# Chunk attention and phase mixing on one core: three steps moved in the body, and the last tiles' transposes and stores dealt out anew

## The chip, the cores and the metric

The kernel runs on one core of a Trainium2 chip. The metric is device time in microseconds for one execution. Five engines work side by side, each through its own list of instructions in order: TensorE (PE in the profile, its weight loads PEld), VectorE (DVE), ScalarE (ACT), GpSimd (POOL) and SyncE (SP). SP, ACT and POOL can issue DMAs; 16 DMA engines carry them.

## The reference

Attention within chunks of 64 rows, then a mixing layer over the tokens and one over the channels. B = 8, H = 8 heads, S = 576 rows, D = 64, so 512 channels.

```python
scores = scale * np.matmul(q_c, k_c.transpose(0, 1, 2, 4, 3))   # chunks of 64 rows
attn = softmax(scores)
x = np.matmul(attn, v_c)                                        # to [B, S, H * D]
theta = x @ w_theta
zr, zi = x * np.cos(theta), x * np.sin(theta)
y = einsum('ts,bsd->btd', w_tok_r, zr) + einsum('ts,bsd->btd', w_tok_i, zi)
u = x + y
out = u + np.maximum(u @ w_ch, 0.0)
```

Inputs and output are float32; the kernel computes in float16 with float32 sums.

## The kernel before

The eight batches are taken in four pairs p = 0 to 3. A pair has nine tiles of 128 rows: four of its first batch (j = 0 to 3), four of the second (j = 4 to 7), and tile 8 (MID), which holds the last 64 rows of both. For loading and attention the tiles go in groups: A and B are two tiles each of the first batch, C and D of the second, M is tile 8.

All work is cut into steps, and one list, `ORDER`, names them in the order in which they are written out. The list sets each engine's order, since an engine runs its instructions in the order of the list. A step is `kind.pj` or `kind.pG`, with a number behind it for its PSUM bank or buffer slot. `R.32.1` is kind R for pair 3, tile 2, into output buffer 1; `W.38.4` is kind W for pair 3, tile 8, into bank 4. Loads run far ahead of the work of their pair. The kinds that matter here:

- `qk`, `v`: loads of q, k and v, cast to float16 on the way, on POOL's queue (lines 174, 169, 214).
- `T`: 32 by 32 transposes of q and k on DVE (321). `S`: scores on PE (339). `E`: exponential on ACT (365). `V0`, `V1`: attention times v on PE, four heads each (382). `N0`, `N1`: division by the sum on DVE, into x (397, 399).
- `X` and `xa`, `xv`, `xd`: x transposed, by PE with a copy by ACT or DVE, or by a transposing DMA on SP's queue (436).
- `H`: x times w_theta on PE (457), called the phase product here. `G`: cosine and sine on ACT (476). `Z`: zr and zi on DVE (492 to 499).
- `Y`: the mix over tokens on PE, 9 matmuls a tile, 18 for MID (522). `A`: u = x + y on DVE (534).
- `U` and `ua`, `uv`: u transposed by PE into PSUM (539) and copied by ACT (551) or DVE (549). `ud` does the same with one transposing DMA on SP's queue (547).
- `W`: u times w_ch on PE, four matmuls (562), the channel product. For the very last tile it is cut into two halves, W0 and W1. `R`: out = u + max(product, 0) on DVE (574), the sum of the title.
- `st`, `sa`: the store of a tile's output from SP's queue or from ACT's (590; 587 for MID, which takes two DMAs). `st0` and `sa1` store the halves of the last tile.

PSUM has eight banks, used by number. Output buffers o0 to o5 are used by slot: an R that writes slot 4 waits until the store of the R before it in slot 4 has landed. A store issued in order on ACT's or SP's queue waits for its R, and what stands behind it in the queue waits as well.

The end of the list before, from tile 28's store on, shows the order of the stores (ACT's `sa`, SP's `st` and `ud`):

```
sa.33 W.35.5 ud.31.7 ud.38.4 R.35.2 sa.30 sa.28 sa.34 W.36.7 R.36.3 ud.37.2 sa.35 sa.36
W.31.3 R.31.5 W.38.4 R.38.0 W.22.1 R.22.4 sa.31 sa.32 sa.22 W0.37.2 R0.37.2 W1.37.0
st.38 R1.37.3 sa1.37 st0.37
```

Of the kernel before, what the change touches and what calls it, by code (L numbers as in the profile page):

```python
# [17 lines left out]
pre.00 qk.0M.0 hq.0A.1 cqa.0A.2 hk.0A.3 Tq.0M.0 Tk.0M v.0M init.00 v.0A dm.21.7 S.0M.0
E.0M.0 lw.02.4 qk.0B.5 dm.3.7 V1.0M.1 lw.01.6 v.0B ckv.0A lw.00.7 qk.0C.8 Tq.0A.1 Tk0.0A
Tk1.0A dm.1.7 S0.0A.2 S1.0A.4 E0.0A.1 lw.03.9 v.0C qk.0D.10 v.0D E1.0A lc.00 qk.1A.11  # L20
v.1A N1.0M dm.1.7 V0.0A.6 N0.0A V0.0M.0 V1.0A.1 N1.0A dm.3.5 TW.02.3 lt.00.12 X0.0A.5
lt.01.1 twv.02 X1.0A.6 xv0.0A.0 cta.01 xv1.0A cta.00 dm.2.7 H0.0A.7 Tq.0B.2 Tk0.0B
Tk1.0B N0.0M H1.0A.1 S1.0B.2 G0.0A.0 G1.0A Z0.0A dm.1.7 S0.0B.4 Z1.0A TW.01.6 X.0M.0
Ya.02.1 xv.0M.1 twv.01 E0.0B.2 V0.0B.4 N0.0B qk.1M.0 E1.0B V1.0B.6 N1.0B H.0M.0 Ya.01.2
X0.0B.3 X1.0B.4 TW.00.5 xv0.0B.2 G.0M.1 xa1.0B H0.0B.7 H1.0B.0 Tq.0C.0 G0.0B.2 G1.0B
Tk.0C S.0C.3 twv.00 Ya.00.7 Z0.0B TW.03.5 Z1.0B Z.0M Yb.02 Ym.02 E.0C.3 Yb.00 Ym.00 A.02
Yb.01 Tq.0D.1 V1.0C.3 twa.03 A.00 V0.0C.0 Ym.01 Ya.03.5 Tk.0D N1.0C S.0D.6 U.02.3 N0.0C
ua.02.0 qk.1B.3 Yb.03 v.1M lw.04.2 X.0C.4 A.01 U.01.0 Ym.03 qk.1C.1 U.00.1 v.1B E.0D.0
A.03 V1.0D.2 N1.0D ua.01.1 qk.1D.4 qk.2M.12 v.1D V0.0D.6 xa.0C.3 v.2D qk.2C.5 v.1C
W.02.0 N0.0D H.0C.4 U.03.2 ua.00.2 G.0C.0 T.1A.2 W.00.3 R.00.0 X.0D.1 S.1A.6 xv.0D.0  # L30
E.1A.1 v.2B qk.2A.6 W.01.3 H.0D.4 v.2M V0.1A.6 R.02.1 V1.1A.0 R.01.2 Ym.07.3 uv.03.3
G.0D.2 Ym.06.2 Z.0C N1.1A Ya.07 Ym.04.0 Ya.04 Ya.06 N0.1A W.03.1 X.1A.6 xa.1A.1 Z.0D
Yb.06 T.1M.0 Yb.04 TW.04.4 R.03.3 twa.04 T.1B.1 S.1M.7 st.02 E.1M.2 A.04 A.06 S.1B.0
Yb.07 H.1A.4 V1.1M.6 qk.3M.7 qk.2B.8 v.2A A.07 N1.1M E.1B.3 V1.1B.2 st.01 V0.1B.0 N0.1B
Y.08.7 V0.1M.6 N1.1B G.1A.1 U.06.0 ua.06.4 Ym.05.1 N0.1M X.1B.4 st.00 U.04.5 Ya.05
U.07.2 X.1M.3 xa.1B.2 A.08 T.1D.2 xv.1M.3 ua.04.5 H.1B.6 H.1M.0 v.3A qk.3A.9 ua.07.6
W.07.4 qk.3B.10 T.1C.0 G.1B.0 v.2C S.1C.2 S.1D.5 U.08.7 Yb.05 Z.1A Z.1B G.1M.2 Z.1M
uv.08.7 R.07.4 Y.12.0 E.1D.0 Y.11.7 v.3M A.12 E.1C.1 A.05 qk.3C.11 V0.1D.4 T.2M.1
V1.1D.2 V0.1C.0 Y.13.6 N1.1D W.08.2 N0.1D U.12.3 N0.1C A.11 X.1D.4 R.08.5 st.03 uv.12.0
T.2A.0 Y.10.5 A.10 A.13 V1.1C.0 S.2M.7 v.3C qk.2D.0 S.2A.2 N1.1C U.11.5 st.07 uv.11.2  # L40
W.06.6 st.08 X.1C.0 W.04.1 xa.1D.0 H.1D.4 E.2A.3 E.2M.2 R.04.1 U.05.2 xa.1C.1 T.2B.2
G.1D.1 H.1C.0 uv.05.1 T.2C.1 W.05.3 Z.1D st.04 R.05.2 S.2B.4 V1.2M.7 G.1C.0 Z.1C V0.2M.2
E.2B.0 sa.05 N1.2M W.11.3 U.10.0 ua.10.3 Y.17.1 N0.2M R.11.0 R.06.3 A.17 Y.15.7 V0.2B.4
V0.2A.2 A.15 N0.2B N0.2A V1.2B.0 Y.18.6 A.18 S.2C.4 sa.11 X.2M.7 xv.2M.2 W.10.2 N1.2B
R.10.4 E.2C.1 T.3M.0 H.2M.3 Y.16.6 U.13.7 G.2M.2 X.2B.4 V1.2A.0 A.16 st.06 st.10 uv.13.6
xa.2B.3 V0.2C.2 V1.2C.5 N1.2A N1.2C N0.2C W.13.7 R.13.5 sa.13 X.2A.4 xd.2C.0 xv.2A.1
H.2B.0 U.18.5 U.17.6 U.16.2 uv.16.7 U.15.3 Y.14.7 ua.18.4 T.2D.2 Z.2M ua.17.5 ua.15.1
W.16.4 H.2A.5 G.2B.1 S.3M.2 S.2D.0 Z.2B G.2A.0 W.12.3 E.3M.2 R.16.1 A.14 Z.2A U.14.4
W.18.7 R.12.2 R.18.0 Y.21.5 Y.23.6 E.2D.0 st.18 V0.2D.2 T.3C.1 A.21 ua.14.2 v.3B T.3A.0
V1.2D.0 qk.3D.3 N1.2D N0.2D T.3B.2 sa.12 S.3A.4 W.14.7 sa.16 A.23 xd.2D.2 H.2C.0 E.3A.3  # L50
R.14.3 Y.22.4 G.2C.2 V0.3M.5 V1.3M.2 T.3D.0 A.22 Z.2C N1.3M st.14 S.3B.6 E.3B.1 S.3C.0
H.2D.3 E.3C.0 N0.3M W.15.6 Y.20.7 v.3D G.2D.1 ud.23.3 R.15.4 V0.3B.0 V0.3A.5 V1.3A.2
Z.2D A.20 W.17.4 R.17.5 N0.3B Y.24.7 Y.27.4 N1.3A N0.3A A.27 V1.3B.0 xd.3M.3 N1.3B st.15
A.24 V1.3C.2 N1.3C S.3D.5 Y.28.4 V0.3C.0 ud.20.6 E.3D.2 V0.3D.5 V1.3D.2 A.28 H.3M.7
N0.3C N0.3D N1.3D xd.3A.1 G.3M.0 ud.27.7 W.27.4 Y.25.0 xd.3B.0 H.3A.5 A.25 ud.22.0
Y.26.1 G.3A.2 H.3B.2 ud.21.4 st.17 A.26 R.27.0 xd.3C.2 G.3B.1 H.3C.5 Z.3A W.21.7 xd.3D.3
Z.3M ud.24.2 G.3C.2 Z.3B R.21.2 Z.3C H.3D.0 Y.33.4 W.24.2 Y.31.3 sa.21 R.24.1 A.33
G.3D.0 Z.3D Y.32.5 st.27 Y.34.6 A.34 Y.36.7 st.24 ud.25.1 W.25.0 A.32 A.36 ud.33.5
W.33.1 ud.26.7 R.33.3 W.20.2 W.23.4 W.26.6 A.31 R.23.4 R.25.5 ud.32.4 W.32.5 Y.30.7
sa.23 R.20.0 Y.38.1 Y.35.3 ud.34.2 sa.25 R.26.2 R.32.1 W.34.4 A.30 sa.20 A.35 st.26  # L60
ud.28.1 ud.36.5 W.28.0 R.34.4 ud.30.6 ud.35.3 A.38 W.30.2 R.30.5 R.28.0 Y.37.6 A.37
sa.33 W.35.5 ud.31.7 ud.38.4 R.35.2 sa.30 sa.28 sa.34 W.36.7 R.36.3 ud.37.2 sa.35 sa.36
W.31.3 R.31.5 W.38.4 R.38.0 W.22.1 R.22.4 sa.31 sa.32 sa.22 W0.37.2 R0.37.2 W1.37.0
st.38 R1.37.3 sa1.37 st0.37
""".split()


# [1 line left out]
def kernel(  # L69
# [500 lines left out]
    def relu_add(f):  # L570
        def last(p, j, slot):
            ps = st.pop(("ps_w", p, j, f))
            o = buffer([P, DM], "o", slot, FP32)[:, 0 : ps.shape[1]]
            nc.vector.scalar_tensor_tensor(  # L574
                out=o, in0=ps, scalar=0.0, in1=st["x", p][:, j, cols[f]],
                op0=ALU.max, op1=ALU.add,
            )
# [4 lines left out]
    def store(queue, f):
        def put(p, j):
            o = st.pop(("o", p, j, f))
            if j == MID:
                for b in range(2):
                    queue.dma_start(out[2 * p + b, KT * P : S, :], o[half[b]])
            else:
                t0 = (j % KT) * P
                queue.dma_start(out[2 * p + j // KT, t0 : t0 + P, cols[f]], o)  # L590

        return put
# [66 lines left out]
```

## Time and profile before

| | |
|---|---|
| median of 3 runs | 194.25 us (192.99 to 195.4) |
| the profiled execution | 192.63 us, of it 190.9 us from the first to the last instruction (the span) |
| PE busy | 179.3 us, 94% of the span |
| DVE busy | 136.8 us, 72% |
| ACT busy | 100.7 us, 53% |
| POOL busy | 84.9 us, 44%, all of it before 115 us |
| granted TensorE clock | 0.999 |
| DMA moved | 31.48 MB, mean 165 GB/s |

A row of the timeline gives the start and length in us, the engine, the line of the kernel, the operation, what it writes and reads, and how many instructions stand in the row; in brackets, how long the engine was idle before it and what ended that. An engine name with a q (SPq, ACTq) is its sequencer, issuing a DMA. A row of one source line gives the shortest, median and longest duration in ns, and a last line the time of its DMAs from issue to landing. The chain of waits is followed back from the last instruction.

### The profile page before, as it was taken

To read this page: it belongs to the slowest core of one execution; us is meant where nothing else is said; L and a number is where in the kernel's file an instruction comes from. 1 tells how busy PE (TensorE), PEld (TensorE's weight loads), DVE (VectorE), ACT (ScalarE), POOL (GpSimd) and SP (SyncE) were. 2 spreads that over 40 slices of the span, in tenths; PEclk is the share of its full clock that TensorE was granted. 3 is DMA by queue.
4 is the path that set the end of the run, shared out by engine and by line. 5 is a ranking of instruction groups with operands and counts; after the bars stand their busy time and mean duration, and the time that the engine had idled before them with its cause. 6 is when DMAs were issued, how large, how long until landed. Compare 5 with 4: busy or idle time off the path is not lost.

```text
span 190.9 us, 6053 instructions
## 1 busy us (share of the span) xinstructions
PE 179.3 (94%) x2626; PEld 93.0 (49%) x2626; DVE 136.8 (72%) x254; ACT 100.7 (53%) x129; POOL 84.9 (44%) x119
## 2 busy tenths in 40 slices
PE   7769899999999999998999999999989999999980
...
DMA  5999999999999999999999998632498315256596
GB/s 156 252 225 187 176 172 174 193 132 159 259 199 162 120 162 198 183 173 194 201 228 200 176 163 180 85 86 82 84 87 177 99 55 137 59 192 165 133 319 213
DMA packets 99867, 31.48 MB, mean 165 GB/s; under 512 B 90880, under 2 KB 94848, under 8 KB 99840
## 3 DMA queue, kind: packets, MB, share of 16 engines
...
q8 instruction: 20, 0.33, 0.7%
q14 instruction: 7, 0.06, 0.1%
...
## 4 chain that ended last, share of the span: by engine, by line
PE 64%; DMA 17%; POOL 6%; ACT 5%; DVE 3%; issue 3%; DVEq 0%; POOLq 0%
PE psum L522 29%; DMA land<-in_k_dram 15%; PE psum L562 12%; PE psum L457 11%; PE psum L339 4%; POOL v L214 3%; PE psum L382 2%; POOL land L174 2%; DMA uT<-x 2%; PE psum L419 2%; PE psum L539 2%; ACT L144 1%; PE psum L288 1%; DVE T L321 1%; ACT sin L476 1%
## 5 line engine op out<-in xcount | busy, mean ns | idle before, releaser
L522 PEld LDWEIGHTS <-wT 128*128 128x128 f16 (+1 forms) x360 | 31.0, 100 | 34.5 <-issue 1.2
L214 POOL DMA_DIRECT2D v<-in_v_dram x56 | 42.0, 772 | 7.1 <-DMA land<-in_k_dram 4.0
L522 PE MATMUL psum<-zr,wT 128*128 128x512 f16 (+1 forms) x180 | 44.7, 380 | 0.0
L522 PE MATMUL psum<-zi,wT 128*128 128x512 f16 (+1 forms) x180 | 42.9, 379 | 0.0
L534 DVE TENSOR_TENSOR x<-psum,x 128x512 f16<-128x512 f32 x36 | 24.3, 684 | 20.2 <-PE psum L522 20.0
L562 PE MATMUL psum<-wch,uT 128*128 128x512 f16 (+1 forms) x148 | 35.2, 374 | 1.2 <-DMA uT<-x 0.7
L457 PE MATMUL psum<-wtheta,xT 128*128 128x512 f16 x144 | 34.1, 379 | 0.2 <-DVE xT L442 0.2
L321 DVE STREAM_TRANSPOSE T<-land 128x1024 f32<-128x1024 f32 (+4 forms) x27 | 25.4, 953 | 10.0 <-DMA land<-in_q_dram 5.9
L574 DVE SCALAR_TENSOR_TENSOR o<-psum,x 128x512 f32<-128x512 f32 (+1 forms) x37 | 24.1, 670 | 9.3 <-PE psum L562 9.2
L365 ACT ACTIVATE eT<-psum 128x1024 f16<-128x1024 f32 (+1 forms) x22 | 18.2, 860 | 22.7 <-PE psum L339 20.3
L476 ACT ACTIVATE cos<-psum,pihalf 128x1024 f16<-128x1024 f32 (+1 forms) x22 | 21.1, 958 | 12.5 <-PE psum L457 11.4
L399 DVE TENSOR_TENSOR x<-psum,recip 128x512 f16<-128x512 f32 (+1 forms) x40 | 25.5, 638 | 1.4
L144 ACT ACT_TABLE_LOAD x20 | 25.7, 1283 | 1.1 <-PEq L643 0.7
L562 PEld LDWEIGHTS <-uT 128*128 128x128 f16 x148 | 13.6, 98 | 15.8 <-DMA uT<-x 1.5
L457 PEld LDWEIGHTS <-xT 128*128 128x128 f16 x144 | 13.5, 98 | 16.0 <-DVE xT L442 0.6
L476 ACT ACTIVATE sin<-psum 128x1024 f16<-128x1024 f32 (+1 forms) x22 | 19.0, 865 | 0.0
L174 POOL DMA_DIRECT2D land<-in_q_dram x15 | 14.3, 950 | 5.8 <-DMA land<-in_k_dram 2.1
L339 PE MATMUL psum<-T 32*64 32x64 f16 x1152 | 13.7, 193 | 3.3 <-DVE T L321 3.3
L339 PEld LDWEIGHTS <-T 32*64 32x64 f16 x1152 | 11.8, 106 | 7.6 <-DVE T L321 4.3
L174 POOL DMA_DIRECT2D land<-in_k_dram x15 | 13.6, 907 | 1.7 <-DMA land<-in_k_dram 1.5
L492 DVE TENSOR_TENSOR zr<-x,cos 128x1024 f16<-128x1024 f16 (+1 forms) x18 | 11.2, 623 | 1.3 <-ACT cos L476 1.0
L493 DVE TENSOR_TENSOR zi<-x,sin 128x1024 f16<-128x1024 f16 (+1 forms) x18 | 11.3, 627 | 0.8 <-ACT sin L476 0.7
...
## 6 DMA issues: line engine op xcount, KB each, us to landing
...
```

The source lines that it names most:

```text
L144: nc.scalar.activation(out=first, in_=pihalf, func=func)
L174: nc.gpsimd.dma_start(t[:, w].rearrange("p h s d -> p h (s d)"), ap[2 * p + bb, :, s0 : s0 + GT, :].rearrange("h (p s) d -> p h (s d)", s=2),)
L214: nc.gpsimd.dma_start(v16[rows, slot + t, :, 0:D], v[b, :, t0 : t0 + m, :].rearrange("h s d -> s h d"),)
L321: nc.vector.transpose(to.bitcast(FP32).rearrange("p (x l s) -> p x s l", l=32, s=2), src.bitcast(FP32).rearrange("p (x s d) -> p x s d", s ...
L339: nc.tensor.matmul(ps[half[r ^ cc], r, h - hs[0]], t[quarter[c], 1, h, :, e], t[quarter[c], 0, h, :, e], start=(e == 0), stop=(e == 1), ti ...
L399: nc.vector.tensor_tensor(out=x.rearrange("p r (h d) -> p r h d", h=H // 2), in0=ps[:, :, :, 0:D], in1=recip[:, 0:n].broadcast_to((P, n, H ...
L457: nc.tensor.matmul(ps[:, (j - js[0]) * DM : (j - js[0] + 1) * DM], xT[:, j, a, :], wtheta16[:, a, :], start=(a == 0), stop=(a == NDB - 1),)
L476: nc.scalar.activation(out=t[:, js[0] : js[-1] + 1].rearrange("p j e -> p (j e)"), in_=ps, func=AF.Sin, bias=bias, scale=1.0,)
L522: nc.tensor.matmul(ps[half[c]] if j == MID else ps, wT[:, kt, t0 : min(t0 + P, S)], z, start=(b is not None and i == 0), stop=(i == len(kt ...
L534: nc.vector.tensor_tensor(out=x, in0=st.pop(("ps_y", p, j)), in1=x, op=ALU.add)
L562: nc.tensor.matmul(ps, uT[:, a, :], wch16[:, a, cols[f]], start=(a == 0), stop=(a == NDB - 1),)
L574: nc.vector.scalar_tensor_tensor(out=o, in0=ps, scalar=0.0, in1=st["x", p][:, j, cols[f]], op0=ALU.max, op1=ALU.add,)
```

## The change

No step computes anything else than before; the order, three places and some issuers change:

- `R.06.3` stands behind `R.04.1` rather than behind `R.11.0`, and `W.11` writes bank 6 rather than bank 3.
- `H.3M.7` stands ahead of `V0.3C`, `V0.3D` and `V1.3D` rather than behind them.
- Tile 37: `ud.37.2` is gone; `U.37.0` on PE and `ua.37.2` on ACT do its work, behind `W.36`.
- `W.22` stands ahead of `W.38`, and R.22 ahead of R.38.
- Stores: 33, 32, 34, 30 and 28 go from ACT's queue to POOL's (`sg`), each right behind its R or one W later; 35 and 31 go from ACT's to SP's (`st`); the two DMAs of 38 go to SP's and ACT's (`sx`); 36, 22 and the halves of 37 stay where they were.

```diff
-... U.05.2 ... W.11.3 U.10.0 ua.10.3 Y.17.1 N0.2M R.11.0 R.06.3 A.17 ...
+... R.06.3 U.05.2 ... W.11.6 U.10.0 ua.10.3 Y.17.1 N0.2M R.11.0 A.17 ...
-... Y.28.4 V0.3C.0 ud.20.6 E.3D.2 V0.3D.5 V1.3D.2 A.28 H.3M.7 N0.3C ...
+... Y.28.4 H.3M.7 V0.3C.0 ud.20.6 E.3D.2 V0.3D.5 V1.3D.2 A.28 N0.3C ...
+W.25.0 A.32 A.36 ud.33.5 W.33.1 ud.26.7 R.33.3 W.20.2 W.23.4 sg.33 W.26.6 A.31 R.23.4 R.25.5
+ud.32.4 W.32.5 Y.30.7 sa.23 R.20.0 Y.38.1 Y.35.3 ud.34.2 sa.25 R.26.2 R.32.1 sg.32 W.34.4 A.30
+sa.20 A.35 st.26 ud.28.1 ud.36.5 W.28.0 R.34.4 sg.34 ud.30.6 ud.35.3 A.38 W.30.2 R.30.5 sg.30
+R.28.0 sg.28 Y.37.6 A.37 W.35.5 ud.31.7 ud.38.4 R.35.2 st.35 W.36.7 U.37.0 ua.37.2 R.36.3 sa.36
+W.31.3 R.31.5 st.31 W.22.1 W.38.4 R.22.4 sa.22 R.38.0 sx.38 W0.37.2 R0.37.2 st0.37 W1.37.0
+R1.37.3 sa1.37
@@
-    def store(queue, f):
+    def store(queue, f, second=None):
         def put(p, j):
             o = st.pop(("o", p, j, f))
             if j == MID:
-                for b in range(2):
-                    queue.dma_start(out[2 * p + b, KT * P : S, :], o[half[b]])
+                for b, q in enumerate((queue, second or queue)):
+                    q.dma_start(out[2 * p + b, KT * P : S, :], o[half[b]])
@@
+        "sg": store(nc.gpsimd, None), "sx": store(nc.sync, None, nc.scalar),
```

More of the change, by code (lines that the diff above doesn't have):

```diff
@@ L17 @@
 ORDER = """
[L18 to L64, printed above, removed]
+pre.00 qk.0M.0 hq.0A.1 cqa.0A.2 hk.0A.3 Tq.0M.0 Tk.0M v.0M init.00 v.0A dm.21.7 S.0M.0 E.0M.0
+lw.02.4 qk.0B.5 dm.3.7 V1.0M.1 lw.01.6 v.0B ckv.0A lw.00.7 qk.0C.8 Tq.0A.1 Tk0.0A Tk1.0A dm.1.7
@@ new lines @@
+S0.0A.2 S1.0A.4 E0.0A.1 lw.03.9 v.0C qk.0D.10 v.0D E1.0A lc.00 qk.1A.11 v.1A N1.0M dm.1.7
+V0.0A.6 N0.0A V0.0M.0 V1.0A.1 N1.0A dm.3.5 TW.02.3 lt.00.12 X0.0A.5 lt.01.1 twv.02 X1.0A.6
+xv0.0A.0 cta.01 xv1.0A cta.00 dm.2.7 H0.0A.7 Tq.0B.2 Tk0.0B Tk1.0B N0.0M H1.0A.1 S1.0B.2 G0.0A.0
+G1.0A Z0.0A dm.1.7 S0.0B.4 Z1.0A TW.01.6 X.0M.0 Ya.02.1 xv.0M.1 twv.01 E0.0B.2 V0.0B.4 N0.0B
+qk.1M.0 E1.0B V1.0B.6 N1.0B H.0M.0 Ya.01.2 X0.0B.3 X1.0B.4 TW.00.5 xv0.0B.2 G.0M.1 xa1.0B
+H0.0B.7 H1.0B.0 Tq.0C.0 G0.0B.2 G1.0B Tk.0C S.0C.3 twv.00 Ya.00.7 Z0.0B TW.03.5 Z1.0B Z.0M Yb.02
@@ new lines @@
+Ym.02 E.0C.3 Yb.00 Ym.00 A.02 Yb.01 Tq.0D.1 V1.0C.3 twa.03 A.00 V0.0C.0 Ym.01 Ya.03.5 Tk.0D
+N1.0C S.0D.6 U.02.3 N0.0C ua.02.0 qk.1B.3 Yb.03 v.1M lw.04.2 X.0C.4 A.01 U.01.0 Ym.03 qk.1C.1
+U.00.1 v.1B E.0D.0 A.03 V1.0D.2 N1.0D ua.01.1 qk.1D.4 qk.2M.12 v.1D V0.0D.6 xa.0C.3 v.2D qk.2C.5
+v.1C W.02.0 N0.0D H.0C.4 U.03.2 ua.00.2 G.0C.0 T.1A.2 W.00.3 R.00.0 X.0D.1 S.1A.6 xv.0D.0 E.1A.1
+v.2B qk.2A.6 W.01.3 H.0D.4 v.2M V0.1A.6 R.02.1 V1.1A.0 R.01.2 Ym.07.3 uv.03.3 G.0D.2 Ym.06.2
+Z.0C N1.1A Ya.07 Ym.04.0 Ya.04 Ya.06 N0.1A W.03.1 X.1A.6 xa.1A.1 Z.0D Yb.06 T.1M.0 Yb.04 TW.04.4
@@ new lines @@
+R.03.3 twa.04 T.1B.1 S.1M.7 st.02 E.1M.2 A.04 A.06 S.1B.0 Yb.07 H.1A.4 V1.1M.6 qk.3M.7 qk.2B.8
+v.2A A.07 N1.1M E.1B.3 V1.1B.2 st.01 V0.1B.0 N0.1B Y.08.7 V0.1M.6 N1.1B G.1A.1 U.06.0 ua.06.4
+Ym.05.1 N0.1M X.1B.4 st.00 U.04.5 Ya.05 U.07.2 X.1M.3 xa.1B.2 A.08 T.1D.2 xv.1M.3 ua.04.5 H.1B.6
+H.1M.0 v.3A qk.3A.9 ua.07.6 W.07.4 qk.3B.10 T.1C.0 G.1B.0 v.2C S.1C.2 S.1D.5 U.08.7 Yb.05 Z.1A
+Z.1B G.1M.2 Z.1M uv.08.7 R.07.4 Y.12.0 E.1D.0 Y.11.7 v.3M A.12 E.1C.1 A.05 qk.3C.11 V0.1D.4
+T.2M.1 V1.1D.2 V0.1C.0 Y.13.6 N1.1D W.08.2 N0.1D U.12.3 N0.1C A.11 X.1D.4 R.08.5 st.03 uv.12.0
@@ new lines @@
+T.2A.0 Y.10.5 A.10 A.13 V1.1C.0 S.2M.7 v.3C qk.2D.0 S.2A.2 N1.1C U.11.5 st.07 uv.11.2 W.06.6
+st.08 X.1C.0 W.04.1 xa.1D.0 H.1D.4 E.2A.3 E.2M.2 R.04.1 R.06.3 U.05.2 xa.1C.1 T.2B.2 G.1D.1
+H.1C.0 uv.05.1 T.2C.1 W.05.3 Z.1D st.04 R.05.2 S.2B.4 V1.2M.7 G.1C.0 Z.1C V0.2M.2 E.2B.0 sa.05
+N1.2M W.11.6 U.10.0 ua.10.3 Y.17.1 N0.2M R.11.0 A.17 Y.15.7 V0.2B.4 V0.2A.2 A.15 N0.2B N0.2A
+V1.2B.0 Y.18.6 A.18 S.2C.4 sa.11 X.2M.7 xv.2M.2 W.10.2 N1.2B R.10.4 E.2C.1 T.3M.0 H.2M.3 Y.16.6
+U.13.7 G.2M.2 X.2B.4 V1.2A.0 A.16 st.06 st.10 uv.13.6 xa.2B.3 V0.2C.2 V1.2C.5 N1.2A N1.2C N0.2C
@@ new lines @@
+W.13.7 R.13.5 sa.13 X.2A.4 xd.2C.0 xv.2A.1 H.2B.0 U.18.5 U.17.6 U.16.2 uv.16.7 U.15.3 Y.14.7
+ua.18.4 T.2D.2 Z.2M ua.17.5 ua.15.1 W.16.4 H.2A.5 G.2B.1 S.3M.2 S.2D.0 Z.2B G.2A.0 W.12.3 E.3M.2
+R.16.1 A.14 Z.2A U.14.4 W.18.7 R.12.2 R.18.0 Y.21.5 Y.23.6 E.2D.0 st.18 V0.2D.2 T.3C.1 A.21
+ua.14.2 v.3B T.3A.0 V1.2D.0 qk.3D.3 N1.2D N0.2D T.3B.2 sa.12 S.3A.4 W.14.7 sa.16 A.23 xd.2D.2
+H.2C.0 E.3A.3 R.14.3 Y.22.4 G.2C.2 V0.3M.5 V1.3M.2 T.3D.0 A.22 Z.2C N1.3M st.14 S.3B.6 E.3B.1
+S.3C.0 H.2D.3 E.3C.0 N0.3M W.15.6 Y.20.7 v.3D G.2D.1 ud.23.3 R.15.4 V0.3B.0 V0.3A.5 V1.3A.2 Z.2D
@@ new lines @@
+A.20 W.17.4 R.17.5 N0.3B Y.24.7 Y.27.4 N1.3A N0.3A A.27 V1.3B.0 xd.3M.3 N1.3B st.15 A.24 V1.3C.2
+N1.3C S.3D.5 Y.28.4 H.3M.7 V0.3C.0 ud.20.6 E.3D.2 V0.3D.5 V1.3D.2 A.28 N0.3C N0.3D N1.3D xd.3A.1
+G.3M.0 ud.27.7 W.27.4 Y.25.0 xd.3B.0 H.3A.5 A.25 ud.22.0 Y.26.1 G.3A.2 H.3B.2 ud.21.4 st.17 A.26
+R.27.0 xd.3C.2 G.3B.1 H.3C.5 Z.3A W.21.7 xd.3D.3 Z.3M ud.24.2 G.3C.2 Z.3B R.21.2 Z.3C H.3D.0
+Y.33.4 W.24.2 Y.31.3 sa.21 R.24.1 A.33 G.3D.0 Z.3D Y.32.5 st.27 Y.34.6 A.34 Y.36.7 st.24 ud.25.1
+W.25.0 A.32 A.36 ud.33.5 W.33.1 ud.26.7 R.33.3 W.20.2 W.23.4 sg.33 W.26.6 A.31 R.23.4 R.25.5
```

## The prediction

> **What bounds the kernel now.** I read the page first: the busy shares, the DMA line, and the chain that ended last.
>
> ```profile
> PE 179.3 (94%) x2626; PEld 93.0 (49%) x2626; DVE 136.8 (72%) x254; ACT 100.7 (53%) x129; POOL 84.9 (44%) x119
> ...
> DMA  5999999999999999999999998632498315256596
> GB/s 156 252 225 187 176 172 174 193 132 159 259 199 162 120 162 198 183 173 194 201 228 200 176 163 180 85 86 82 84 87 177 99 55 137 59 192 165 133 319 213
> ...
> PE 64%; DMA 17%; POOL 6%; ACT 5%; DVE 3%; issue 3%; DVEq 0%; POOLq 0%
> ```
>
> TensorE (PE) carries 64% of the chain. The DMA engines are full for the first 24 of 40 slices (the loads), and again in the last four (transposes and stores). One slice is 4.77 us. I then cut the second half into stretches with the view by windows (columns: stretch and its length, busy us and count of PE, PE's weight loads, DVE, ACT, POOL, then clock, DMA share, GB/s).
>
> ```profile
> 131.00:157.00 26.00, 25.34 (x262) 12.02 (x260) 18.08 (x37) 12.54 (x15) 0.00 (x0) 1.00 0.52 97
> ...
> 182.00:186.00 4.00, 3.29 (x20) 1.54 (x17) 2.61 (x5) 0.00 (x0) 0.00 (x0) 1.00 1.03 349
> 186.00:190.00 4.00, 0.14 (x2) 0.00 (x0) 0.65 (x2) 0.00 (x0) 0.00 (x0) 1.00 0.80 262
> ```
>
> From 131 us PE has no slack except what these 26 us show (0.66 us). From 182 us the bound changes: PE is idle for 0.7 us, and the DMA engines run full at 349 GB/s. The clock is 1.00 throughout, and POOL does nothing. The chain of the last microseconds and its timeline say which wait ends last.
>
> ```profile
> 179.33 3.98 DMA uT<-x
> ...
> 183.36 1.92 PE psum L562 x8
> ```
>
> ```profile
> 167.79 3.08 DVE L574 SCALAR_TENSOR_TENSOR o<-psum,x 128x512 f32<-128x512 f32 x5 [0.44 <-PE psum L562]
> ...
> 176.29 5.75 SPq L547 DMA_TRANSPOSE uT<-x  x4
> ...
> 178.16 1.29 DVE L574 SCALAR_TENSOR_TENSOR o<-psum,x 128x512 f32<-128x512 f32 x2 [0.44 <-PE psum L562]
> ...
> 179.90 2.75 PE L562 MATMUL psum<-wch,uT 128*128 128x512 f16 x12
> ...
> 180.81 6.22 ACTq L590 DMA_DIRECT2D out_dram<-o  x7
> ...
> 183.36 2.77 PE L562 MATMUL psum<-wch,uT 128*128 128x512 f16 x16 [0.71 <-DMA uT<-x]
> 184.59 2.06 DVE L574 SCALAR_TENSOR_TENSOR o<-psum,x 128x512 f32<-128x512 f32 x4 [1.21 <-PE psum L562]
> ...
> 186.65 0.59 SPq L590 DMA_DIRECT2D out_dram<-o  x1
> ```
>
> By the order, the twelve matmuls at 179.90 are W.35, W.36, W.31; the sixteen at 183.36 are W.38, W.22, W0.37, W1.37. W.38 waits for its transposed tile (ud.38, issued 179.33, landed 183.31). The last R ends at 184.59 + 2.06 = 186.65, SP sends st0.37 then, and the landing takes 3.1 us (row below): 189.75, plus 1.1 us of closing, is the span of 190.9. The seven stores at 180.81 on ACT's queue are 34, 35, 36, 31, 32, 22 and half of 37. Tile 32's result was the last of the five R ending at 170.87, but its store stands fifth in this row: it waits 13 us behind others, and adds its bytes to the full stretch.
>
> **The change part by part.** Body, first place: R.06 moves up behind R.04, and W.11 uses bank 6, which R.06 frees, in place of bank 3, which R.05 frees.
>
> ```profile
> 82.50 0.69 DVE L574 SCALAR_TENSOR_TENSOR o<-psum,x 128x512 f32<-128x512 f32 x1 [1.45 <-PE psum L562]
> 83.97 1.25 DVE L321 STREAM_TRANSPOSE T<-land 128x1024 f32<-128x1024 f32 x1 [0.78 <-DMA land<-in_k_dram]
> ...
> 87.76 0.69 DVE L574 SCALAR_TENSOR_TENSOR o<-psum,x 128x512 f32<-128x512 f32 x1
> 88.36 0.68 DVE L492 TENSOR_TENSOR zr<-x,cos 128x1024 f16<-128x1024 f16 x1
> ```
>
> ```profile
> 88.50 1.02 PE L562 MATMUL psum<-wch,uT 128*128 128x512 f16 x4 [0.49 <-DVE o L574]
> ```
>
> ```profile
> 83.22 9.09 SPq L590 DMA_DIRECT2D out_dram<-o  x2
> ```
>
> DVE: R.04 is the 82.50 row; R.06 behind it needs 0.6 us (five R in 3.08 us: (3.08 - 0.69) / 4) and fits into the 0.78 us in which DVE waits for a landing. Cost nothing; without that cover 0.6 us. PE: W.11's 0.49 us wait for R.05 (87.76 + 0.69) goes. The next product, Y.17, would come 0.49 us earlier at about 89.09, and its first phase input ends at 88.36 + 0.68 = 89.04: just in time. How far does it carry? DVE waits for a landing again:
>
> ```profile
> 107.06 1.25 DVE L321 STREAM_TRANSPOSE T<-land 128x1024 f32<-128x1024 f32 x1 [0.67 <-DMA land<-in_k_dram]
> ...
> 111.75 0.68 DVE L534 TENSOR_TENSOR x<-psum,x 128x512 f16<-128x512 f32 x1
> ...
> 112.65 0.39 PE L539 MATMUL psum<-id,x 128*128 128x128 f16 x4
> ```
>
> From that landing DVE runs without a break to A.14 (111.75 to 112.43), which U.14 on PE needs at 112.65. So only some 0.2 us of the 0.49 survive; I take 0.15, bounds 0 and 0.49. R.06 also issues a store later: st.06 is second in the SP row (ending 92.3) and would go out at about 83.8, since nothing is ahead of it on SP. Its 256 KB then compete with loads 8 us earlier, at 173 to 194 GB/s up to 1.4 us for them. The next landing that DVE waits for is the one at 107.06, and the bytes before that are the same; I take 0, bounds 0.3 either way.
>
> Body, second place: H.3M goes ahead of V0.3C, V0.3D, V1.3D.
>
> ```profile
> 138.84 0.51 PE L382 MATMUL psum<-v,eT 64*64 64x65 f16 x40
> 139.97 0.26 PE L382 MATMUL psum<-v,eT 64*64 64x65 f16 x8 [0.62 <-issue]
> 140.16 1.04 PE L457 MATMUL psum<-wtheta,xT 128*128 128x512 f16 x4
> ```
>
> ```profile
> q8 instruction: 20, 0.33, 0.7%
> ```
>
> PE's work is unchanged (four matmuls), but the 0.62 us stop is not a wait for data: it falls in the middle of V1.3D, and the view gives "issue". The burst runs 40 matmuls in 0.51 us, and queue q8 brings 20 pieces of instructions for 5252 PE entries (2626 loads and matmuls each), about 260 to a piece. I read it as PE running out of instructions. Four slow matmuls ahead of the burst give 0.87 us, more than the stop. Bounds: 0 (it moves along) and 0.62; I take 0.6, since the row is no semaphore wait and the added time covers it. The three V's N's come 0.9 us later on DVE; their users are SP's transposes several us on. The Trainium skill, "Runtime: NRT & Kernel Launch", section "Instruction fetch mechanics", says instructions arrive in 16 KiB blocks of 256 whose boundaries are mostly hidden; by that the stop has another cause, and this term is 0.
>
> The end: tile 37's u goes through PE and ACT rather than through SP's transposing DMA.
>
> ```profile
> 105.10 1.06 PE L539 MATMUL psum<-id,x 128*128 128x128 f16 x16
> ```
>
> ```profile
> L551 ACT COPY uT<-psum x11: 577/587/603, 36.5 to 115.6; 128x512 f16<-128x512 f16 x11
> ```
>
> Four transposes cost PE 0.22 us (1.06 less one matmul's 0.22, over 15, times 4). The copy is 0.59 us on an ACT that has no other work; behind it sa.36 waits, no longer than R.36 makes it wait anyway. U.37 needs A.37, done at 180.79 in time for U.37's place at 181.63. W.22 now goes before W.38, so PE has work while ud.38 lands. On PE: the next slot after W.31 was 182.50 (12 matmuls, 0.216 us each), W.38 began at 183.36; 0.86 lost, less 0.22, is 0.64 us gained: W.31 at 181.85, W.22 182.71, W.38 183.57, W1.37 done at about 185.5.
>
> Stores: 33, 32, 34, 30, 28 go to POOL's queue. No trace row shows a store from POOL; these rows bound its landing.
>
> ```profile
> L214 POOL DMA_DIRECT2D v<-in_v_dram x56: 679/730/950, 3.7 to 107.3; - x56
> ...
> DMA to landing us min/median/max: 3.8/6.6/11.2
> ```
>
> ```profile
> L590 ACTq DMA_DIRECT2D out_dram<-o x8: 338/378/691, 178.9 to 186.7; - x8
> ...
> DMA to landing us min/median/max: 2.7/3.4/4.0
> ```
>
> ```profile
> L590 SPq DMA_DIRECT2D out_dram<-o x1: 591/591/591, 186.6 to 186.6; - x1
> ...
> DMA to landing us min/median/max: 3.1/3.1/3.1
> ```
>
> From 2.7 us (as fast as ACT's) to 11.2 us (POOL's slowest load). I take 4.5, nearest to POOL's fastest 3.8: the loads ran on a full queue, the stores find it empty. It matters, because output buffers come free only on landing: R.31 needs sg.30's, R.22 needs sg.34's, R.38 needs both of sg.28's. R.30 and R.28 end at 178.85 and 179.45; with 0.73 us an issue, the second half of sg.28 is issued at 180.33 and lands at 184.85. R.38 would be ready at 184.6, so it starts at 184.9; R0.37 and R1.37 follow at 0.6 and 0.3 us, and R1.37 ends at 186.25, where before it was 186.65. The store behind it lands in about 2.7 us rather than 3.1, as 0.5 MB (32 and 34) and one 128 KB transpose have left the full stretch: 188.95 against 189.75. Gain 0.8 us. The bounds are +1.5 (3.8 us, no gate, landing 2.3) and a loss (below). The Trainium skill, "DMA: Bandwidth & Descriptors", section "Anatomy of one DMA — SWDGE (gpsimd) path", gives about 2.0 us plus bytes at 436 GB/s; the estimate for 256 KB is 2.6 us, and by it no buffer is late and the tail gains 1.3. No row of POOL here is that fast.
>
> Sum: 0.15 + 0.6 + 0.8 = 1.55 us off the profiled execution's 192.63 us (span 190.9 and 1.7 around it): 191.1, a ratio of 0.992. That execution is 0.8% below the median shown, 194.25; times 0.992 this is 192.7.
>
> **The rivals.** (a) POOL's stores land late, and the result is slower. Every us beyond 4.2 delays R.38, R0.37, R1.37 by one. With the median 6.6: sg.28 lands at 186.95, R1.37 ends at 188.3, its store at 191.3: 1.5 us later than before, 0.8 with the body's 0.75 taken off; 195.0 (with 11.2: 5.4 us, 199.7). It decides from about 5.8 us on. For it: the median is that; against: those loads have small packets on a saturated queue.
>
> (b) The bytes set the end, not the order, and the body's gains are absorbed. DMA share is 1.03 in 182 to 186; then only what the store queues waited counts, some 0.3 us: 193.9. Against it: the 13 us wait of store 32. The Trainium skill's "Issuing engines are not separate DMA queues", in "DMA: Bandwidth & Descriptors", says that spreading over issuers only saves their issue time; by that alone this would be the result.
>
> (c) The early stores slow the transposes.
>
> ```profile
> L547 SPq DMA_TRANSPOSE uT<-x x2: 1222/1222/1222, 179.3 to 180.8; - x2
> ...
> DMA to landing us min/median/max: 4.0/4.1/4.2
> ```
>
> Beside stores a transpose took 4.1 us; ud.31, third of the four from 176.29 (issued about 178.0, now beside sg.34), would land at 182.1, 0.25 us behind W.31's place. At most twice that with ud.30, which takes 0.5 us off the gain: 193.2.
>
> (d) All bounds fall well: 0.49 + 0.6 + 1.5 = 2.6: 191.6.
>
> (e) The moved H.3M only moves the stop, R.06 gains nothing: the tail's 0.8 alone: 193.4.
>
> **How the numbers follow.** Chances: forecast 0.43, (a) 0.15, (b) 0.15, (c) 0.10, (d) 0.09, (e) 0.08. The range 191.2 to 195.1 takes in (b) to (e) and (a) at its median, and leaves out (a)'s far end and luck beyond (d). 2% is 3.9 us, about what a measurement of this kernel can tell from no change: no case but (a) near POOL's slowest gets there, so slower 0.06, faster 0.04, same 0.90.
>
> **What would show it.** PE's 0.49 us before W.11 gone, and U.14 still released by DVE; no "issue" stop in V1.3D; no idle PE between W.31 and W.38; sg landings near 4.5 us; R.38 starting at its buffer's release rather than at its product's end. I am wrong if sg landings exceed 5.8 us, if R.31 waits for sg.30 by more than half a us, or if the stop stands elsewhere in the burst.

## The result, and the profile after

The changed kernel takes 193.29 us (median of 21 runs, 191.55 to 195.67), the kernel before 194.37 us (21 runs, 192.99 to 195.4). The ratio is 0.9937, with a 95% interval of 0.9914 to 0.996. The forecast was 192.7 us, a ratio of 0.992, inside 191.2 to 195.1. It is a gain of 0.6%: well under the 2% that the prediction names as about what can be told from no change, but the interval of the ratio leaves no change out. The ratios here and below leave out executions more than 1.5% above the fastest of their kernel (3 of the 21 of the changed kernel, 6 of 12 of the kernel called "changed, ud.37 back" below), so a ratio is not the quotient of two medians.

The profiled execution of the changed kernel is not a typical one: its span is 192.3 us, longer than the 190.9 us shown of before, mostly because the clock was granted lower early on. So stretches are compared here, not spans. First the page of the changed kernel (busy shares, the clock in 40 slices, the DMA engines, the chain):

```profile
PE 180.6 (94%) x2630; PEld 93.8 (49%) x2630; DVE 137.0 (71%) x254; ACT 101.2 (53%) x130; POOL 88.2 (46%) x125
...
PEclk9966999999999999999999999999999999999999
DMA  5999999999999999999999996542479217366693
...
PE 80%; DMA 6%; ACT 6%; DVE 3%; issue 1%; POOL 1%; DVEq 0%; POOLq 0%
```

The slices marked 6 are 10 to 19 us. The view by windows (stretch, length, busy us and count of PE, its weight loads, DVE, ACT, POOL, then clock, DMA share, GB/s) gives the clock there:

```profile
10.00:15.00 5.00, 3.74 (x80) 2.07 (x84) 3.16 (x7) 0.60 (x1) 4.73 (x6) 0.57 1.61 215
```

By 88 us PE is 2.4 us behind the kernel before (W.05 starts at 88.36, before at 85.97); 0.4 us of this was there when the first scores started (11.26 against 10.87), which wait for the first load. From there on each stage can be read.

Around W.11 the timeline of PE (changed kernel) shows no wait, and DVE has R.04 and R.06 in one row of two:

```profile
89.96 0.44 PE L378 MATMUL psum<-v,eT 64*64 64x65 f16 x16
90.33 1.04 PE L558 MATMUL psum<-wch,uT 128*128 128x512 f16 x4
```

```profile
84.89 1.29 DVE L570 SCALAR_TENSOR_TENSOR o<-psum,x 128x512 f32<-128x512 f32 x2 [1.45 <-PE psum L558]
86.09 1.24 DVE L317 STREAM_TRANSPOSE T<-land 128x1024 f32<-128x1024 f32 x1
...
108.06 1.24 DVE L317 STREAM_TRANSPOSE T<-land 128x1024 f32<-128x1024 f32 x1
```

The 108.06 row is T.2D, which waited 0.67 us for a landing before. Here it waits for nothing: this execution is late, the loads are not. W.11 comes 1.83 us later than before (90.33 against 88.50) where W.05 came 2.39 later, and PE keeps these 0.56 us. That they come from the move is not shown: T.2B (86.09) did not wait for its landing here, and in executions where it does not, W.11 does not wait in bank 3 either (the sum alone, below).

The burst of V's behind H.3M (timeline of PE, changed kernel):

```profile
140.60 1.04 PE L453 MATMUL psum<-wtheta,xT 128*128 128x512 f16 x4
141.57 0.76 PE L378 MATMUL psum<-v,eT 64*64 64x65 f16 x48
142.27 0.61 PE L558 MATMUL psum<-wch,uT 128*128 128x512 f16 x2
```

All 48 matmuls stand in one row of 0.76 us: the stop of 0.62 us is gone but for a rest. Without any stop the burst takes 0.58 us (H.3M alone, below); here the starts of its 36th and 37th matmul lie 0.18 us apart, 4 earlier in the burst than the old place, as the four matmuls of H.3M now stand ahead of it. W.27 follows at 142.27, 1.23 us later than before, where Y.28 was 1.76 later. So 0.53 us came from here.

At the end nothing is gained. The chain in order of time, the timeline of PE, of DVE, and the row of ud.38's line, all of the changed kernel:

```profile
179.36 1.50 PE psum L518 x7
180.86 4.86 DMA uT<-x
...
185.76 1.93 PE psum L558 x12
```

```profile
182.86 0.39 PE L535 MATMUL psum<-id,x 128*128 128x128 f16 x4
183.09 1.89 PE L558 MATMUL psum<-wch,uT 128*128 128x512 f16 x8
185.76 1.91 PE L558 MATMUL psum<-wch,uT 128*128 128x512 f16 x12 [0.78 <-DMA uT<-x]
```

```profile
181.34 0.69 DVE L530 TENSOR_TENSOR x<-psum,x 128x512 f16<-128x512 f32 x1 [0.65 <-PE psum L518]
...
186.84 1.35 DVE L570 SCALAR_TENSOR_TENSOR o<-psum,x 128x512 f32<-128x512 f32 x3 [1.13 <-PE psum L558]
```

```profile
L543 SPq DMA_TRANSPOSE uT<-x x1: 1224/1224/1224, 180.9 to 180.9; - x1
...
DMA to landing us min/median/max: 4.9/4.9/4.9
```

U.37 costs 0.23 us on PE as said, and W.22 (second half of the row of eight) fills PE. But ud.38 now takes 4.86 us, where it took 3.98, and W.38 waits for it longer than W.22 can cover. (ud.31 takes 3.73 us, where it took 2.58, and lands at 183.00, just ahead of W.31's 183.09.) A.37 starts at 181.34 and the last R ends at 186.84 + 1.35 = 188.19, 6.85 us later; before it was 186.65 - 180.10 = 6.55. The last landing comes 9.82 us after A.37, before 9.64. R.38 is released by its product (PE, L558), not by a buffer: the stores from POOL were not the ones that came late.

```profile
L586 POOL DMA_DIRECT2D out_dram<-o x4: 540/548/586, 168.3 to 180.4; - x4
...
DMA to landing us min/median/max: 2.3/2.9/3.8
```

### The profile page after: what moved, and what is told of

It is laid out like the page before. It is cut to its first block, busy times and chain, and to the rows that moved or that the text cites. A ratio compares the mean times of both kernels' runs of the same rounds, so it can differ in the third digit from the quotient of the medians.

```text
span 192.3 us, 6066 instructions
## 1 busy us (share of the span) xinstructions
PE 180.6 (94%) x2630; PEld 93.8 (49%) x2630; DVE 137.0 (71%) x254; ACT 101.2 (53%) x130; POOL 88.2 (46%) x125
## 4 chain that ended last, share of the span: by engine, by line
PE 80%; DMA 6%; ACT 6%; DVE 3%; issue 1%; POOL 1%; DVEq 0%; POOLq 0%
PE psum L518 34%; PE psum L453 15%; PE psum L558 14%; PE psum L335 6%; DMA land<-in_k_dram 4%; PE psum L378 4%; DMA uT<-x 3%; PE psum L415 2%; PE psum L535 2%; ACT L140 2%; PE psum L154 2%; ACT cos L472 1%; ACT eT L361 1%; ACT sin L472 1%; PE psum L284 1%
## 5 line engine op out<-in xcount | busy, mean ns | idle before, releaser
L558 PE MATMUL psum<-wch,uT 128*128 128x512 f16 (+1 forms) x148 | 35.4, 374 | 0.8 <-DMA uT<-x 0.8
L586 POOL DMA_DIRECT2D out_dram<-o x4 | 2.2, 556 | 70.0 <-DVE o L570 70.0
L547 ACT COPY uT<-psum 128x512 f16<-128x512 f16 x12 | 6.8, 591 | 31.8 <-PE psum L535 31.8
L558 PEld LDWEIGHTS <-uT 128*128 128x128 f16 x148 | 13.5, 98 | 14.9 <-DMA uT<-x 1.3
L335 PE MATMUL psum<-T 32*64 32x64 f16 x1152 | 14.4, 197 | 4.0 <-DVE T L317 4.0
L335 PEld LDWEIGHTS <-T 32*64 32x64 f16 x1152 | 12.6, 109 | 8.5 <-DVE T L317 4.5
```

Of the source, the lines that this page charges most:

```text
L335: nc.tensor.matmul(ps[half[r ^ cc], r, h - hs[0]], t[quarter[c], 1, h, :, e], t[quarter[c], 0, h, :, e], start=(e == 0), stop=(e == 1), ti ...
L558: nc.tensor.matmul(ps, uT[:, a, :], wch16[:, a, cols[f]], start=(a == 0), stop=(a == NDB - 1),)
```

## The experiments

All are compared with the kernel before, which ran beside them. Times in this table are from the traces, between starts of steps: Y.28 to Y.25 holds the burst of V's, A.37 to the end of R1.37 and to the last landing hold the tail. The stretch between Y.25 and A.37 took 38.2 us in every kernel.

| kernel | ratio (95%) | Y.28 to Y.25 | ud.38 | A.37 to R1.37's end | A.37 to last landing |
|---|---|---|---|---|---|
| before | 1 | 5.12 | 3.98 | 6.55 | 9.64 |
| changed | 0.9937 (0.9914 to 0.996) | 4.60 | 4.86 | 6.85 | 9.82 |
| sum alone | 1.0013 (0.9982 to 1.0043) | 5.42 | 3.42 | 6.74 | 10.05 |
| H.3M alone | 0.9942 (0.9911 to 0.9973) | 4.43 | 4.03 | 6.60 | 9.72 |
| tail alone | 0.9999 (0.997 to 1.0028) | 5.16 | 4.74 | 6.71 | 9.65 |
| both of the body | 0.9989 (0.9953 to 1.0026) | 4.42 | 3.84 | 6.85 | 9.80 |
| changed without the sum | 0.9928 (0.9897 to 0.9959) | 4.64 | 4.81 | 6.85 | 9.82 |
| changed, U.38 too | 0.9953 (0.992 to 0.9987) | 4.63 | none | 6.12 | 9.66 |
| changed, ACT for POOL | 0.9951 (0.9916 to 0.9986) | 4.42 | 3.81 | 6.53 | 9.46 |
| changed, ud.37 back | 0.9978 (0.9939 to 1.0016) | 4.42 | 3.84 | 7.99 | 9.74 |
| U.38, then 38 ahead of 22 | 0.9954 (0.9919 to 0.9989) | 4.42 | none | 6.17 | 9.26 |
| U.38, then 22 early | 0.991 (0.9872 to 0.9948) | 4.42 | none | 6.38 | 9.27 |
| before, 33 idle matmuls | one execution | 4.31 | 3.98 | 6.55 | 9.69 |

**The sum alone.**

```diff
 (in the list before)
-... R.04.1 U.05.2 ... W.11.3 ... R.11.0 R.06.3 ...
+... R.04.1 R.06.3 U.05.2 ... W.11.6 ... R.11.0 ...
```

> The kernel before with R.06 behind R.04 and W.11 in bank 6 alone. Theory: PE's 0.49 us wait before W.11 is gone; where PE is ahead of the loads, DVE's wait for qk.2D's landing keeps U.14 in its place and 0.15 to 0.2 us are left in the time (0.1%); where PE is late, all 0.5 us stay (0.25%). Rival (the store that is issued 8 us earlier slows loads): DVE waits longer than 0.67 us for a landing at T.2D, and the time is the same or up to 0.3 us longer.

No wait before W.11, and no change of the time: 0.1% less lies within the interval, the 0.25% of a late execution does not. The rival's longer wait at T.2D is not there (none in this trace). Two things lie behind the result. The wait of 0.49 us is itself the result of a late landing. Of the five kernels with W.11 in bank 3, only two wait before it: before (0.49 us) and H.3M alone (0.71 us), and in both T.2B had waited for its landing (0.78 and 1.00 us). In the tail alone T.2B did not wait, and W.11 follows its predecessor at once (timeline of PE):

```profile
88.05 0.44 PE L377 MATMUL psum<-v,eT 64*64 64x65 f16 x16
88.43 1.04 PE L557 MATMUL psum<-wch,uT 128*128 128x512 f16 x4
```

And the stop in V1.3D was longer here, 0.91 us (timeline of PE):

```profile
141.10 0.52 PE L377 MATMUL psum<-v,eT 64*64 64x65 f16 x40
142.53 0.26 PE L377 MATMUL psum<-v,eT 64*64 64x65 f16 x8 [0.91 <-issue]
```

This execution had the same low clock early, so it cannot show the absorption by T.2D's landing. With both body moves, on an execution that was less late, DVE waited at T.2D again (first row, timeline of DVE), and U.14, which needs A.14, started 0.13 us later than before, measured against the steps ahead of it. The same wait was 1.93 us in the kernel with tile 38 ahead of 22 (last experiment), and there U.14 waited 0.94 us for DVE (second row, timeline of PE). So a gain that comes ahead of T.2D can be lost again at U.14.

```profile
107.43 1.25 DVE L316 STREAM_TRANSPOSE T<-land 128x1024 f32<-128x1024 f32 x1 [0.96 <-DMA land<-in_k_dram]
```

```profile
113.48 0.40 PE L534 MATMUL psum<-id,x 128*128 128x128 f16 x4 [0.94 <-DVE x L529]
```

**H.3M alone.**

```diff
-... Y.28.4 V0.3C.0 ud.20.6 E.3D.2 V0.3D.5 V1.3D.2 A.28 H.3M.7 ...
+... Y.28.4 H.3M.7 V0.3C.0 ud.20.6 E.3D.2 V0.3D.5 V1.3D.2 A.28 ...
```

> The kernel before with H.3M ahead of V0.3C alone. Theory (PE runs out of instructions in the burst): the 0.62 us stop in V1.3D is gone and Y.25 comes 0.5 to 0.6 us earlier against Y.28 (5.12 us from start to start before, so 4.5 to 4.6); the time falls by 0.5 us, 0.25%. Rival (the stop only moves): a stop of 0.4 us or more stands in V0.3C or V0.3D, Y.28 to Y.25 stays 5.0 to 5.2 us, and the time stays.

As the theory expected: 4.43 us from Y.28 to Y.25 and no stop in the burst (timeline of PE). The time fell by more than the 0.25% expected, by 0.58%, and the interval just leaves 0.25% out. It is within noise of the whole change's: one moved step of four matmuls is enough for the result here.

```profile
140.41 1.04 PE L452 MATMUL psum<-wtheta,xT 128*128 128x512 f16 x4
141.38 0.58 PE L377 MATMUL psum<-v,eT 64*64 64x65 f16 x48
```

**The tail alone.** The list before up to Y.26, the changed list from there on.

> The kernel before with the new list from Y.26 on (stores, U.37, W.22 ahead of W.38), the body as before. Theory (early stores slow the transposing DMA of tile 38): ud.38 takes 4.5 to 5 us, PE idles 0.5 us or more before W.38, and the time from A.37 to the last landing stays within 0.3 us of the 9.6 us of before: ratio 0.998 to 1.002. Rival (the tail gains what was predicted): ud.38 lands before W.22 ends, and 0.6 to 0.9 us are gone, ratio 0.996. Rival (stores from POOL land late): their landing takes over 5.8 us, R.38 waits for its buffer, ratio above 1.002.

The first theory holds in each number: ud.38 4.74 us, PE idle 0.64 us before W.38, the last landing 9.65 us after A.37 (9.64 before), ratio 0.9999. Its reason, the early stores, is not shown: 30's and 28's stores were issued beside ud.38 before, too, and 33's and 32's have landed here when ud.38 is issued.

```profile
184.75 1.91 PE L557 MATMUL psum<-wch,uT 128*128 128x512 f16 x12 [0.64 <-DMA uT<-x]
```

**Both moves of the body**, with the tail of before.

> The kernel before with both body moves (R.06 with W.11, and H.3M), and its own tail. Theory (the whole difference comes from the body, most of it from H.3M): no wait before W.11, no stop in V1.3D, and the ratio is that of the changed kernel, 0.992 to 0.996. Rival (the tail brings a part): 0.997 or more. If R.06's 0.5 us carries through, 0.25% below the kernel with H.3M alone (0.994), so 0.9915; if it does not, 0.994.

The trace agrees with the theory (no wait before W.11, 4.42 us from Y.28 to Y.25). The time does not: 0.9989 lies in the range of the rival. Its interval holds both 0.996 and 1.002 and overlaps with that of H.3M alone, so the pair is not shown to differ from it; nor does it confirm. Why it came out smaller is open.

**The changed kernel without the sum** (H.3M and the new tail).

> The changed kernel with R.06 behind R.11 and W.11 in bank 3 as before, so H.3M and the new tail only. Theory (R.06's 0.5 us is absorbed by DVE's wait for the landing of qk.2D, and the tail gives nothing): ratio as with H.3M alone and as the changed kernel, 0.993 to 0.996; from Y.28 to Y.25 4.4 to 4.6 us. Rival (R.06 brings what the changed kernel has beyond H.3M): 0.997 or above.

0.9928: R.06 and W.11 bring nothing that can be measured, here too.

**Idle matmuls to shift PE's instructions.**

```diff
-... v.0A dm.21.7 S.0M.0 ...
+... v.0A dm.33.7 S.0M.0 ...
```

> The kernel before with 33 rather than 21 idle matmuls ahead of the first scores, nothing else; they only fill the wait for the first load, and what follows is the same work 24 PE entries later in PE's instructions. Theory (PE runs out of instructions at a block's end, and the next block is there some 2.3 us after its transfer on q8 began): the stop moves 12 matmuls ahead, so 28 rather than 40 matmuls of the burst run before it, inside V0.3D; it ends 2.2 to 2.4 us after the start of the q8 transfer near it. Rival (the stop belongs to V1.3D, by a bank or an operand): it stays after 40.

The stop left V1.3D, which it should not by the rival, since neither bank nor operand changed. It did not go where the theory put it: the burst near 139 us ran 48 matmuls without a stop, and Y.28 to Y.25 took 4.31 us without the moved step. Instead one of 1.24 us stands in an earlier burst, where the kernel before had none (timeline of PE):

```profile
139.54 0.58 PE L377 MATMUL psum<-v,eT 64*64 64x65 f16 x48
```

```profile
37.91 0.41 PE L377 MATMUL psum<-v,eT 64*64 64x65 f16 x27
39.56 0.23 PE L377 MATMUL psum<-v,eT 64*64 64x65 f16 x5 [1.24 <-issue]
```

The q8 transfers give the rule that was missing. They start at 137.70 us (before), 140.14 (sum alone), 138.06 (tail alone) and 37.23 (this run); the stops end at 139.97, 142.53, 140.35 and 39.56. That is 2.27, 2.39, 2.29 and 2.33 us later. The DMA view of a tenth of a microsecond, 37.2 to 37.3 us of the shifted kernel, shows such a transfer:

```profile
q8 instruction: 1, 0.02, 59.1%
```

Counted over PE's weight loads and matmuls that had started, 4801 entries lie ahead of each of the three late stops and 1217 ahead of the early one, 3584 or 14 times 256 fewer. Shorter stops in other kernels fit in: 0.21 to 0.27 us at 1217 entries in three of them, and 0.16 to 0.68 us at 3265, which is 6 times 256 fewer than 4801, in five. They ended 2.4 to 2.6 us after a transfer on q8 began. The longest of them, in the kernel with ud.37 back (timeline of PE):

```profile
98.53 0.27 PE L414 MATMUL psum<-id,x 128*128 128x128 f16 x2 [0.68 <-issue]
```

No other stop of PE over 0.15 us without a releaser stands in the thirteen traces. All this fits blocks of 256 entries, each of which can be used some 2.3 to 2.6 us after its transfer begins; PE stops if it gets there sooner. How long the stop at one place is differs from trace to trace. In this run the transfer near the late burst began at 135.39 us, early enough; the one at 37.23 was not. Why a transfer begins when it does is open.

**Tile 38's u by TensorE too.**

```diff
 (in the changed list)
-... W.35.5 ud.31.7 ud.38.4 R.35.2 ...
+... W.35.5 U.38.1 ua.38.4 ud.31.7 R.35.2 ...
```

> The changed kernel, with tile 38's u by TensorE and ScalarE too (U.38 and ua.38 behind W.35 in place of ud.38). Theory (W.38 waits for a slowed transpose): PE has no idle time between W.35 and W1.37 but 0.22 us more work; R1.37 ends about 0.5 us earlier against A.37 than in the changed kernel (6.85 us there, so 6.2 to 6.5 us), and the time is 0.3 to 0.7 us under the changed kernel, ratio to the kernel before 0.990 to 0.992. Rival (bytes of the stores set the end): R1.37 ends earlier, but the last landing does not follow, ratio 0.993 to 0.995 as the changed kernel.

PE has no idle time any more: the last twenty matmuls stand in one row.

```profile
182.56 3.63 PE L557 MATMUL psum<-wch,uT 128*128 128x512 f16 x20
```

R1.37 ends 6.12 us after A.37, 0.73 us earlier than in the changed kernel. But the last landing does not follow: the store sa1.37 is issued at 187.02 and lands 3.23 us later, 9.66 us after A.37.

```profile
L585 ACTq DMA_DIRECT2D out_dram<-o x1: 457/457/457, 187.0 to 187.0; - x1
...
DMA to landing us min/median/max: 3.2/3.2/3.2
```

The time is near the rival's, 0.9953. The mechanism of the wait was right; that it is what the time waits for was wrong. The rival's reason, the bytes, is not borne out either. In the stretches from 4 to 6 and from 6 to 8 us after A.37 the DMA engines were full before (share 1.06 and 1.02, the last but one number of the first two rows), and they are not in this kernel (0.70 and 0.79, the other two):

```profile
184.10:186.10 2.00, 2.00 (x14) 1.06 (x12) 1.49 (x3) 0.00 (x0) 0.00 (x0) 1.00 1.06 406
186.10:188.10 2.00, 0.04 (x1) 0.00 (x0) 0.55 (x2) 0.00 (x0) 0.00 (x0) 1.00 1.02 335
```

```profile
184.59:186.59 2.00, 1.60 (x12) 0.89 (x10) 1.89 (x4) 0.00 (x0) 0.00 (x0) 1.00 0.70 261
186.59:188.59 2.00, 0.00 (x0) 0.00 (x0) 0.12 (x1) 0.00 (x0) 0.00 (x0) 1.00 0.79 223
```

**ACT's queue in place of POOL's.** `sg.33`, `sg.32`, `sg.34`, `sg.30`, `sg.28` become `sa` at the same places.

> The changed kernel with the five stores of POOL's queue issued from ACT's queue at the same places. Theory (any store beside a transposing DMA slows it): ud.38 still takes 4.5 to 5 us, PE still idles 0.5 us or more before W.38, ratio to the kernel before 0.992 to 0.996. Rival (POOL's queue is what slows it): ud.38 lands within 4.0 us, the idle time before W.38 is under 0.1 us, R1.37 ends 0.6 us earlier against A.37 than the 6.85 us of the changed kernel, ratio about 0.991.

Each theory in part. ud.38 took 3.81 us and W.38 did not wait, as the rival said; the ratio, 0.9951, is in the range of the theory. But ud.31, the transpose ahead of it, took 4.4 us (178.09 to 182.49) and PE waited for that one, before W.31:

```profile
182.53 3.64 PE L557 MATMUL psum<-wch,uT 128*128 128x512 f16 x20 [0.46 <-DMA uT<-x]
```

Which queue sends the stores makes no difference that can be measured in the time: 0.9951 against 0.9937, intervals overlapping.

**Tile 37 by the DMA again.** `U.37.0` out, `ud.37.2` in place of `ua.37.2`.

> The changed kernel with tile 37's u by the transposing DMA again (no U.37, no ua.37), all else as changed. Theory (transposes beside stores take 4.5 us and more): ud.37, issued behind ud.38, lands at 6 us or later after A.37, W0.37 waits for it, R1.37 ends 7.0 to 7.6 us after A.37, and the time is 0.2 to 0.7 us above the changed kernel: ratio 0.995 to 0.998. Rival (tile 37's way does not matter since W.38 waits anyway): R1.37 6.6 to 6.9 us after A.37, ratio 0.993.

ud.37 was issued at 182.94 and landed at 187.37 us, 6.4 us after A.37. PE waited 1.94 us for it:

```profile
187.41 1.05 PE L557 MATMUL psum<-wch,uT 128*128 128x256 f16 x8 [1.94 <-DMA uT<-x]
```

R1.37 ends 7.99 us after A.37, above the 7.0 to 7.6 expected, and the ratio, 0.9978, is at the upper end of the theory's. Even so the last landing comes at 9.74, no later than in the others: the stores of 22 and 38 had nearly landed, and the two last ones took 1.7 us each. And ud.38 took 3.84 us here beside the same stores from POOL, not 4.5. In the three traces with the whole new tail it took 4.74 to 4.86 us, in the five with the tail of before 3.42 to 4.03. So it goes with the tail, but POOL's stores alone do not make it slow, and what does is not settled.

**Order of the last tiles.** With U.38, first tile 38 ahead of 22, then tile 22 right behind Y.37.

```diff
-... W.22.1 W.38.4 R.22.4 sa.22 R.38.0 sx.38 W0.37.2 ...
+... W.38.4 R.38.0 sx.38 W.22.1 R.22.4 sa.22 W0.37.2 ...
```

> The changed kernel with U.38 and ua.38 in place of ud.38 as before in this study, and W.38, R.38 with its two stores ahead of W.22, R.22. Theory (with PE never waiting, the last four small stores in one burst are what ends late: 3.5 us from R1.37's end to the last landing against 3.0): R1.37 ends 6.1 us after A.37, the last landing comes 2.9 to 3.2 us later, so 9.0 to 9.3 us after A.37 where it was 9.6 to 9.8 in all kernels so far; ratio to the kernel before 0.990 to 0.993. Rival (the bytes of the last tiles set the end, whatever their order): 9.6 us again, ratio 0.994 to 0.996.

> The changed kernel with U.38 and ua.38 in place of ud.38 and tile 22's product, sum and store right behind Y.37. Theory (what ends last is the burst of small stores behind R.38 and R.37, so it should hold no other store): R1.37 ends 6.1 to 6.2 us after A.37, the last landing 2.3 to 2.9 us later, 8.5 to 9.0 us after A.37 (9.27 with tile 22 between 38 and 37); ratio 0.991 to 0.995. Rival (the burst is no slower than the path of one store): 9.2 to 9.4 us.

Both bring the last landing to 9.26 and 9.27 us after A.37, 0.4 to 0.55 us earlier than the changed tail in other kernels; the first as its theory expected at the slow end, the second against its theory (8.5 to 9.0). The ratios do not follow: the first's, 0.9954, is in the range of its rival, the second's, 0.991, in that of its theory. In the second R1.37 waits for its buffer, which the store of tile 36 frees:

```profile
185.07 1.02 DVE L569 SCALAR_TENSOR_TENSOR o<-psum,x 128x512 f32<-128x512 f32 x2 [0.17 <-PE psum L557]
186.26 0.42 DVE L569 SCALAR_TENSOR_TENSOR o<-psum,x 128x256 f32<-128x256 f32 x1 [0.17 <-DMA out_dram<-o]
```

The second is the fastest kernel tried, 192.26 us and a ratio of 0.991 (0.9872 to 0.9948). It beats the kernel before; that it beats the changed kernel is not shown, as the intervals overlap.

## Why the prediction was right, and where it was not

**The second place of the body (0.6 us) was right, in size and in cause.** Y.28 to Y.25 fell from 5.12, 5.16 and 5.42 us without the move to 4.42 to 4.64 in all kernels with it. The higher of these have a rest of the stop at the 36th matmul of the burst, 0.13 to 0.22 us from start to start, in three kernels: in small, the prediction's sign of being wrong that the stop stands elsewhere in the burst. The reading of "issue" in the middle of a step as PE out of instructions is borne out by the shifted kernel and the 2.3 us. The Trainium skill's section "Instruction fetch mechanics" of "Runtime: NRT & Kernel Launch" has the blocks of 256; the measured stops agree with the size. That their crossing is mostly hidden agrees as well for most of the 20 transfers, and not where a boundary falls into a run of small matmuls or shortly behind one. By the Trainium skill this term would have been 0; the measurement decides otherwise.

**The first place (0.15 us): too small to measure, as forecast.** The wait before W.11 went. That DVE's wait for a landing at T.2D can take a gain back by way of U.14 is shown (0.13 us with both moves, 0.94 us with 38 ahead of 22); that 0.15 us is left is not. What the prediction did not see is that the wait is not a fixed cost of the order: it comes and goes with the landing before T.2B.

**The tail (0.8 us) was wrong: it is 0.** The step that failed is "PE has work while ud.38 lands", with W.38 put at 183.57. That is 3.47 us after A.37; W.38 started 4.42 us after A.37. The prediction took ud.38's 3.98 us as given; it took 4.86 and was issued 0.3 us later against A.37. Rival (c) had the slower transpose and gave it to ud.31 and ud.30. ud.31 did take 3.73 us rather than 2.58, without a wait behind it; ud.38 cost PE 0.78 us. Why it is slower with the new tail stays open. The second error is the one that counts more: the landing of the last store was costed at 2.7 us behind R1.37. The kernel with U.38 had R1.37 as early as forecast, and its last landing 3.5 us behind. The last landing came 9.5 to 10.05 us after A.37 whether R1.37 ended at 6.1 or at 8.0, and only another order of the last stores moved it. Rival (b) said that the end would be set by the stores; its reason, bytes, fits the kernel before, and not the kernel with U.38, whose DMA engines were busy 0.70 and 0.79 of the time there. (That the DMA engines are full again in the last four slices of the page is misread: the digits are 6, 5, 9 and 6. The window from 182 to 186 us, by which the prediction goes on, has 1.03.) What remains open is what holds the four small stores of 38 and 37 when they come together.

**POOL's landing (4.5 us) was too high,** 2.3 to 3.8 for whole tiles and 3.6 to 4.2 for tile 28's halves. So R.38's buffer was free in time, and rival (a) never came near its point of 5.8. The Trainium skill, "DMA: Bandwidth & Descriptors", section "Anatomy of one DMA — SWDGE (gpsimd) path", gave the estimate of 2.6 us for 256 KB; the median of the whole tiles here, 2.9 us, is nearer to it than to the 4.5. But by this estimate the tail would have gained 1.3 us, and it gained nothing.

Of the sum of 1.55 us, 1.2 us came (0.63% of 194.37; the interval is 0.8 to 1.7). The traces, of one execution each, assign 0.5 to 1.0 us of it to the second place of the body (5.12 to 5.42 less 4.42 to 4.64). The sum and the tail alone gave ratios of 1.0013 and 0.9999, so the rest has no step of its own; the intervals of these two leave room for 0.2% and 0.3%. The forecast was right by the middle one of its three terms. That 1.2 us came so near to 1.55 is in part luck, since the 0.8 us of the tail are not in it. By the number alone rivals (c), 193.2 us, and (e), 193.4, were nearer than the forecast's 192.7; but (e) has the gain come from the tail and none from H.3M, and the traces show the reverse.
